# Value sums of the last four chunks moved behind all their scores, values landing in pieces, and wider rows of wo

## Chip, cores, metric

The kernel runs on one core of one Trainium2 chip. The metric is device microseconds, median of several runs. Runs of one kernel agree to about 1 to 3 us of 1955, so a difference of one microsecond needs the trace beside the time, and the profile's span is about 2 us shorter than the time that is quoted.

In the lines of a profile, PE is TensorE's matmuls, PEld the weight loads for them, DVE is VectorE, ACT ScalarE. The chain is the work that ended last, followed back to what released each step. The granted clock is the share of its full clock that PE gets: 1.00 is full, 0.50 half.

## The reference

One token attends with 32 heads of width 192 over a cache of 32,768 keys and values per head, then comes a small dense layer. What matters:

```
q      = layernorm(x) @ wq                      # 32 heads x 192
scores = q . k_cache * 192**-0.5                # k_cache: 32 x 32768 x 192, bf16, 403 MB
p      = softmax(scores)
o      = p . v_cache                            # v_cache: another 403 MB
h      = x + concat(o) @ wo                     # wo: 6144 x 640
out    = h + relu(layernorm(h) @ w1) @ w2
```

Nearly all of the work is to read 825 MB once.

## The kernel before

Keys and values come in loads of 64 rows per partition, each worked off in two chunks of 32. Of each chunk, 20 (or fewer) rows are scored on PE, for which they are transposed and copied out of PSUM by ScalarE; VectorE scores the others. The last head ends with smaller loads of 40, 16 and 8 rows, that is chunks of 20, 20, 16 and 8, called **a, b, c, d** below. The code is shortened: `...` marks what is left out between functions, and lines inside them are left out too.

```python
full = [(JL, [(J, 20), (J, 20)])] * (Sk // (P * JL))
ends = full[:-1] + [(40, [(20, 12), (20, 12)]), (16, [(16, 10)]), (8, [(8, 4)])]
NEND = 3
...
wo_view = A_wo.rearrange("(b p) n -> p b n", p=P)          # rows of 640 bf16 = 1280 B
...
def transposes(g):                                          # PE, then ScalarE
    for b0 in range(0, NB, 8):
        for b in range(nb): nc.tensor.transpose(out=tp[:, b, :], in_=kt[...], identity=ident_b[:])
        nc.scalar.copy(out=kT[:, b0:b0 + nb, :], in_=tp[:, 0:nb, :])
def scores_pe(g):                                           # PE (sp), then exp on ScalarE -> pB
def scores_dve(g):                                          # VectorE; exp_dve(g) makes pA on ScalarE
def pv(g):                                                  # value sums: matmuls with two rows each
    for i, j in enumerate(order):
        nc.tensor.matmul(o[:], lhsT=p, rhs=vt[:, (c0 + j) * Dh:(c0 + j + 2) * Dh], ...)
...
def o_scale(h):    # even heads fill columns 0..191 of o_pair, odd heads 192..383
    nc.vector.tensor_scalar_mul(out=dst[:, 0, n0:n0 + Dh], in0=o[:, 0:Dh], scalar1=s[0:2, 1:2])
    nc.scalar.activation(out=dst[:, 1, n0:n0 + Dh], in_=o[:, Dh:2 * Dh], func=F.Copy, scale=s[0:2, 1:2])
def o_turn(h):     # row -> column, once for two heads
    for b in range(3):
        for i in range(2):
            nc.tensor.matmul(ps[:, b:b + 1], lhsT=src[:, i, b * P:(b + 1) * P], rhs=ident_f[0:2, i:i + 1], ...)
...
for g in range(G):
    ...
    transposes(g)
    if g > 0:
        pv(g - 1)
    scores_pe(g)
    sc = scores_dve(g)
    ...
    exp_dve(g, sc)
den_mm(H - 1); den_rec(H - 1)
pv(G - 1)
o_scale(H - 1); o_turn(H - 1); project(H // 2 - 1)
# layernorm, w1, relu, w2, store
```

So a chunk's value sum stands on PE between the next chunk's transposes and that chunk's scores.

The softmax here doesn't subtract the row's maximum and nothing guards it: scores larger than these inputs give would overflow.

## Time and profile before

| | before |
|---|---|
| time, median of 3 runs | 1954.45 us |
| span of the profiled run | 1952.3 us |
| PE starts on the last full key load (it waits for its landing) | 1912.12 |
| PE starts on a | 1925.38 |
| den product starts (all probabilities are there) | 1939.51 |
| last value sum ends | 1940.65 |
| wo projection starts | 1942.67 |

The rows below the second are read on the timeline of PE, in us. The den product is the matmul that adds up the probabilities of a head, by which the value sums are then divided; the turn (`o_turn`, tile oT_ps) brings two heads' results from rows into columns for wo. The lines that carry the reading are in the prediction: the page shows that the transfers are the bound up to the end, and the chain shows what follows the last of them. The table cuts that end into stages.

### The profile page before, as it was taken

Reading aid. Unit: us, or ns where it says so; the run is one execution under the profiler, and the core shown is the slowest. Engines: PE = TensorE matmul, PEld = TensorE weight load, DVE = VectorE, ACT = ScalarE, POOL = GpSimd, SP = SyncE. Lnnn points to the kernel's source line nnn. Section 1 sums busy time; section 2 is a strip of 40 time slices with the busy share of each in tenths; the row PEclk is TensorE's granted clock in tenths of the full one; section 3 lists DMA queues with packets and bytes.
Section 4 is the critical chain, followed back from the end, with each engine's and each line's share of the span. In section 5 each row is a group of like instructions: output and inputs, shape, how many; then the busy total and the mean of one; then the engine's idle time right before and its main releaser. Section 6 shows DMA issues by size and latency. Waiting matters only on the chain.

```text
span 1952.3 us, 44906 instructions
## 1 busy us (share of the span) xinstructions
PE 1594.4 (82%) x20392; PEld 1122.4 (57%) x20392; DVE 1338.0 (69%) x654; ACT 1067.5 (55%) x2223; POOL 0.7 (0%) x6
## 2 busy tenths in 40 slices
PE   6887887878788788787888877888788887887887
PEld 4655565555556556555555655655555565565655
DVE  5766777667666676676767666777666766676675
ACT  4555555555555555555655555555555555555554
POOL 0000000000000000000000000000000000000000
PEclk9989889989998889998988989899899989898998
DMA  9999999999999999999999999999999999999996
GB/s 405 431 429 429 430 431 430 429 429 431 431 430 428 430 431 430 431 429 431 430 429 430 429 431 430 430 431 424 431 431 428 425 421 431 427 430 426 430 421 253
DMA packets 51522, 827.85 MB, mean 424 GB/s; under 512 B 4612, under 2 KB 17412, under 8 KB 18564
## 3 DMA queue, kind: packets, MB, share of 16 engines
q1 hardware_dynamic: 51332, 824.99, 99.0%
q8 instruction: 159, 2.61, 0.5%
q14 instruction: 31, 0.25, 0.0%
HBM read 824.97 MB, written 0.00 MB: 423 GB/s over the span
## 4 chain that ended last, share of the span: by engine, by line
DMA 77%; PE 17%; ACT 4%; DVE 1%; issue 1%; SPq 0%; ACTq 0%
DMA kt<-in_A_k_cache_dram 75%; PE o_ps L293 8%; PE tp L239 6%; ACT kT L240 3%; DMA vt<-in_A_v_cache_dram 1%; DVE pr L266 1%; PE sp L249 1%; PE sp L253 1%; PE sp L251 1%; PE qps L205 0%; ACT pA L276 0%; ACT pB L256 0%; DVE o_pair L314 0%; PE oT_ps L327 0%; ACT row_e L208 0%
## 5 line engine op out<-in xcount | busy, mean ns | idle before, releaser
L240 ACT COPY kT<-tp 128x1024 bf16<-128x1024 bf16 (+1 forms) x1025 | 905.2, 966 | 343.1 <-PE tp L239 340.2
L266 DVE TENSOR_TENSOR pr<-kt,qb 128x2304 f32<-128x2304 bf16 (+1 forms) x258 | 655.0, 2539 | 483.3 <-DMA kt<-in_A_k_cache_dram 479.9
L239 PE MATMUL tp<-ident_b,kt 128*128 128x128 bf16 x7677 | 599.3, 242 | 342.8 <-DMA kt<-in_A_k_cache_dram 269.7
L239 PEld LDWEIGHTS <-kt 128*128 128x128 bf16 x7677 | 531.1, 110 | 381.2 <-DMA kt<-in_A_k_cache_dram 280.2
L269 DVE TENSOR_REDUCE sc<-pr 128x12 f32<-128x2304 f32 (+1 forms) x258 | 654.3, 2536 | 27.6 <-ACT kT L240 1.4
L293 PE MATMUL o_ps<-vt,pB 128*2 128x384 bf16 x2559 | 498.8, 346 | 2.6 <-DMA vt<-in_A_v_cache_dram 2.6
L293 PEld LDWEIGHTS <-pB 128*2 128x2 bf16 x2559 | 203.8, 87 | 226.9 <-issue 65.9
L256 ACT ACTIVATE pB<-sp 128x20 bf16<-128x20 f32 (+1 forms) x258 | 48.4, 188 | 492.4 <-PE sp L253 492.4
L293 PE MATMUL o_ps<-vt,pA 128*2 128x384 bf16 x1537 | 291.9, 326 | 0.0
L249 PEld LDWEIGHTS <-kT 128*128 128x128 bf16 x2559 | 196.1, 96 | 85.7 <-issue 84.7
L249 PE MATMUL sp<-qm,kT 128*128 128x2 bf16 x2559 | 218.6, 164 | 0.5 <-ACT kT L240 0.5
L251 PE MATMUL sp<-qm,kT 128*128 128x1 bf16 x2559 | 215.0, 163 | 0.0
L253 PE MATMUL sp<-qm,kT 128*128 128x1 bf16 x2559 | 215.0, 163 | 0.0
L251 PEld LDWEIGHTS <-kT 128*128 128x128 bf16 x2559 | 198.7, 96 | 0.0
L293 PEld LDWEIGHTS <-pA 128*2 128x2 bf16 x1537 | 129.1, 84 | 120.8
L253 PEld LDWEIGHTS <-kT 128*128 128x128 bf16 x2559 | 197.4, 96 | 0.0
L276 ACT ACTIVATE pA<-sc 128x12 bf16<-128x12 f32 (+1 forms) x258 | 52.8, 205 | 0.0
L256 ACT ACTIVATION_READ_ACCUMULATOR pB<-sp 128x1 f32 x258 | 50.1, 194 | 0.0
L276 ACT ACTIVATION_READ_ACCUMULATOR pA<-sc 128x1 f32 x258 | 49.3, 191 | 0.0
L305 DVE TENSOR_REDUCE rec<-den 128x1 f32<-128x20 f32 x32 | 5.7, 179 | 60.2 <-PE den L299 60.2
L315 ACT ACTIVATE o_pair<-o_ps,rec 2x192 f32<-2x192 f32 x32 | 13.2, 412 | 26.9 <-DVE o_pair L314 26.9
L327 PE MATMUL oT_ps<-ident_f,o_pair 2*128 2x1 f32 x192 | 24.2, 247 | 0.1
(60 smaller groups left out, 191.4 us busy)
## 6 DMA issues: line engine op xcount, KB each, us to landing
kt<-in_A_k_cache_dram SPq DMA_DIRECT2D x127, 3072.0 KB, 35.7
vt<-in_A_v_cache_dram SPq DMA_DIRECT2D x127, 3072.0 KB, 31.4
wq<-in_A_wq_dram SPq DMA_DIRECT2D x8, 960.0 KB, 34.7
wo<-in_A_wo_dram SPq DMA_DIRECT2D x16, 480.0 KB, 31.2
kt<-in_A_k_cache_dram SPq DMA_DIRECT2D x1, 1920.0 KB, 30.7
vt<-in_A_v_cache_dram SPq DMA_DIRECT2D x1, 1920.0 KB, 25.4
kt<-in_B_w_dram SPq DMA_DIRECT2D x1, 1920.0 KB, 17.1
vt<-in_B_w_dram SPq DMA_DIRECT2D x2, 960.0 KB, 13.3
```

Of the source, the lines that this page charges most:

```text
L239: nc.tensor.transpose(out=tp[:, b, :], in_=kt[:, off:off + P], identity=ident_b[:])
L240: nc.scalar.copy(out=kT[:, b0:b0 + nb, :], in_=tp[:, 0:nb, :])
L249: nc.tensor.matmul(sp[:, 2 * i:2 * i + 2], lhsT=kT[:, 3 * i + 1, :], rhs=qm[:, 1:3], start=True, stop=False, skip_group_check=True)
L251: nc.tensor.matmul(sp[:, 2 * i:2 * i + 1], lhsT=kT[:, 3 * i, :], rhs=qm[:, 0:1], start=False, stop=False, skip_group_check=True)
L253: nc.tensor.matmul(sp[:, 2 * i + 1:2 * i + 2], lhsT=kT[:, 3 * i + 2, :], rhs=qm[:, 3:4], start=False, stop=True, skip_group_check=True)
L256: nc.scalar.activation(out=pB[:, 0:JP], in_=sp[:, 0:JP], func=F.Exp, scale=SCALE, accum_out=dsums[:, h, 2 * c + 1:2 * c + 2])
L266: nc.vector.tensor_tensor(out=pr[:, 0:JD, :], in0=kt[:, c0 * Dh:(c0 + JD) * Dh].rearrange("p (j d) -> p j d", d=Dh), in1=qb[:].unsqueeze(1 ...
L269: nc.vector.reduce_sum(out=sc[:, 0:JD], in_=pr[:, 0:JD, :], axis=mybir.AxisListType.X)
L276: nc.scalar.activation(out=pA[:, 0:JD], in_=sc[:, 0:JD], func=F.Exp, scale=SCALE, accum_out=dsums[:, h, 2 * c:2 * c + 1])
L293: nc.tensor.matmul(o[:], lhsT=p, rhs=vt[:, (c0 + j) * Dh:(c0 + j + 2) * Dh], start=first, stop=last)
L315: nc.scalar.activation(out=dst[:, 1, n0:n0 + Dh], in_=o[:, Dh:2 * Dh], func=F.Copy, scale=s[0:2, 1:2])
L327: nc.tensor.matmul(ps[:, b:b + 1], lhsT=src[:, i, b * P:(b + 1) * P], rhs=ident_f[0:2, i:i + 1], start=(i == 0), stop=(i == 1))
```

## The change

Its intent: no value sum shall make the scores of the last chunks wait, because ScalarE's copies and exponentials need those scores; values come early enough by halves; and wider rows of wo make fewer, cheaper packets. The core of the diff:

```diff
+    ENDS = [g for g in range(G) if chunks[g][2] >= len(loads) - NEND]
-    pcp = ctx.enter_context(tc.tile_pool(name="pcp", bufs=3))
+    pcp = ctx.enter_context(tc.tile_pool(name="pcp", bufs=6))
-    wo_view = A_wo.rearrange("(b p) n -> p b n", p=P)
+    wo_view = A_wo.rearrange("(g p b) n -> g p b n", p=P, b=3)
-        nc.sync.dma_start(out=t[:], in_=wo_view[:, 3 * pr:3 * pr + 3, :])
+        nc.sync.dma_start(out=t[:], in_=wo_view[pr])
 ...                                        (load_part: the load of a and b becomes one DMA for each)
+        for j0, j1 in parts or [(0, jl)]:
+            nc.sync.dma_start(out=t[:, j0 * Dh:j1 * Dh], in_=rows[:, j0 * Dh:j1 * Dh])
 ...                                        (o_turn)
-    nc.tensor.matmul(ps[:, b:b + 1], lhsT=src[:, i, b * P:(b + 1) * P], ...
+    nc.tensor.matmul(ps[:, b:b + 1], lhsT=src[:, i, b:3 * P:3], ...
 ...
-            if g > 0:
+            if g > 0 and g - 1 not in ENDS:
                 pv(g - 1)
 ...
-        pv(G - 1)
+        for g in ENDS:
+            pv(g)
```

A partition now holds three neighbouring rows of wo, so the turn must pick every third column.

More of the change, by code (lines that the diff above doesn't have):

```diff
@@ L112, in load_wo, with load_part @@
         t = wop.tile([P, 3, D], bf16, name="wo")
-        nc.sync.dma_start(out=t[:], in_=wo_view[:, 3 * pr:3 * pr + 3, :])
+        nc.sync.dma_start(out=t[:], in_=wo_view[pr])
         wo_t[pr] = t
-    def load_part(ld, src, pool, tag, name):
+    def load_part(ld, src, pool, tag, name, parts=None):
         h, k0, jl = loads[ld]
@@ L122, in load_part @@
         t = pool.tile([P, size], bf16, tag=tag, name=name)
-        nc.sync.dma_start(out=t[:, 0:jl * Dh], in_=src[h, k0:k0 + P * jl, :].rearrange("(p j) d -> p (j d)", p=P))
+        rows = src[h, k0:k0 + P * jl, :].rearrange("(p j) d -> p (j d)", p=P)
+        for j0, j1 in parts or [(0, jl)]:
+            nc.sync.dma_start(out=t[:, j0 * Dh:j1 * Dh], in_=rows[:, j0 * Dh:j1 * Dh])
         return t
@@ L129, in load_v @@
     def load_v(ld):
-        vt_t[ld] = load_part(ld, v_hd, vpool, "vt", "vt")
+        parts = [(q[3], q[3] + q[4]) for q in chunks if q[2] == ld] if ld >= len(loads) - NEND else None
+        vt_t[ld] = load_part(ld, v_hd, vpool, "vt", "vt", parts)
     w_t = {}
@@ L326, in o_turn @@
                 for i in range(2):
-                    nc.tensor.matmul(ps[:, b:b + 1], lhsT=src[:, i, b * P:(b + 1) * P], rhs=ident_f[0:2, i:i + 1],
+                    nc.tensor.matmul(ps[:, b:b + 1], lhsT=src[:, i, b:3 * P:3], rhs=ident_f[0:2, i:i + 1],
                                      start=(i == 0), stop=(i == 1))
```

## The prediction

> **What bounds the kernel now.** I read the profile page first, for the whole span, and then only the last 60 us, because all but one part of the change touches only those.
>
> ```profile
> DMA  9999999999999999999999999999999999999996
> ...
> q1 hardware_dynamic: 51332, 824.99, 99.0%
> ...
> DMA kt<-in_A_k_cache_dram 75%; PE o_ps L293 8%; PE tp L239 6%; ACT kT L240 3%; DMA vt<-in_A_v_cache_dram 1%; DVE pr L266 1%; PE sp L249 1%; PE sp L253 1%; PE sp L251 1%; PE qps L205 0%; ACT pA L276 0%; ACT pB L256 0%; DVE o_pair L314 0%; PE oT_ps L327 0%; ACT row_e L208 0%
> ```
>
> The reader is to see that the 16 DMA engines are 90% busy or more in every slice but the last, that one queue takes 99% of their time, and that loads of keys make 75% of the chain that ended last. 825 MB must come in, and the engines only have to keep up. So outside the end, only what makes the transfers cheaper can shorten the run. The end is different. I call the last four chunks, of 20, 20, 16 and 8 rows per partition, a, b, c and d. From the chain of work that ended last, in order of time (start, us, what):
>
> ```profile
> 1906.10 25.42 DMA vt<-in_A_v_cache_dram
> 1931.52 0.04 issue
> 1931.56 1.78 PE o_ps L293 x10
> ...
> 1933.88 0.86 PE tp L239 x15
> 1934.74 1.72 PE o_ps L293 x10
> ...
> 1936.91 0.36 PE tp L239 x6
> 1937.27 0.00 issue
> 1937.27 1.46 PE o_ps L293 x8
> ...
> 1939.51 0.40 PE den L299 x2
> 1939.91 0.75 PE o_ps L293 x4
> ```
>
> Their value sums (o_ps) have 10, 10, 8 and 4 matmuls, and all four are in the fence. The first waits until the values of a and b, one transfer, land at 1931.52, but PE had been idle for it only 0.76 us, says the timeline of PE. After it, sums, transposes and scores take turns on PE. The last sum ends at 1940.65 (its last group starts at 1940.16 and takes 0.49), and a chain of small steps from there ends the kernel.
>
> What ScalarE does between is as important (timeline of ScalarE, start, us):
>
> ```profile
> 1930.34 2.21 ACT L240 COPY kT<-tp 128x1024 bf16<-128x1024 bf16 x3
> 1933.92 0.18 ACT L256 ACTIVATE pB<-sp 128x12 bf16<-128x12 f32 x1 [1.38 <-PE sp L253]
> ...
> 1934.44 1.82 ACT L240 COPY kT<-tp 128x1024 bf16<-128x1024 bf16 x2
> 1936.95 0.18 ACT L256 ACTIVATE pB<-sp 128x10 bf16<-128x10 f32 x1 [0.69 <-PE sp L253]
> ...
> 1937.36 0.80 ACT L240 COPY kT<-tp 128x768 bf16<-128x768 bf16 x1
> 1939.01 0.17 ACT L256 ACTIVATE pB<-sp 128x4 bf16<-128x4 f32 x1 [0.84 <-PE sp L253]
> ```
>
> The copies of b, c and d (2.21, 1.82, 0.80 us) must run one after another, each followed by scores on PE and two exponentials, before the next. ScalarE idles only 1.38, 0.69 and 0.84 us before the three exponentials. So the old order already puts the sums of a, b and c largely under the copies of b, c and d.
>
> **What the Trainium skill says.** "TensorE: Matmul & The Clock Gate", section "Part 2: What happens when you issue a matmul": matmuls stay in program order, only weight loads are pulled ahead. So a sum placed after d's scores can't fill a gap before them. The trace agrees: PE sat 0.76 us on the late values with transposes of a later chunk to do. The same page, "Part 1: The HAM clock gate", says that the clock halves after an idle window of about 3.4 us and comes back after a busy one. The trace agrees, with partly idle windows enough (stretch, us; PE busy; later columns include the granted clock):
>
> ```profile
> 1907.00:1910.40 3.40, 1.74 (x36) 1.08 (x34) 0.81 (x1) 0.67 (x5) 0.00 (x0) 0.99 1.00 408
> 1910.40:1917.20 6.80, 5.08 (x36) 3.83 (x37) 4.92 (x2) 3.55 (x4) 0.00 (x0) 0.50 0.78 334
> 1930.80:1934.20 3.40, 2.64 (x38) 1.68 (x38) 3.26 (x3) 2.02 (x7) 0.00 (x0) 1.00 0.91 337
> 1934.20:1937.60 3.40, 3.40 (x44) 2.00 (x42) 2.04 (x3) 2.64 (x9) 0.00 (x0) 1.00 0.95 323
> ```
>
> A stretch with PE busy 1.74 of 3.40 us is followed by half clock (0.50); one with 2.64 of 3.40 is not. "DMA: Bandwidth & Descriptors", section "Why small descriptors are slow (HBM only)", says that each packet has a fixed overhead of about 3 cycles, so small rows lose a little. In the trace's single packets, 1280 B take a median of 55 ns and 3072 B take 121: per byte, the small ones cost 9% more.
>
> **The change part by part.**
>
> 1. Rows of wo. Each of 16 loads goes from 384 packets of 1280 B to 128 of 3840 B; an engine has 24, then 8. By the median packet times, 24 x 55 = 1.32 us, and 8 x 149 = 1.19 us (149 interpolated between 121 for 3072 B and 234 for 6144 B): 0.13 us a load, 2 us in all. But the stream waits for its slowest engine, and in the landing records of the trace a wo load adds 1.17 us to the last engine's landing, against 7.26 us for a load of 3072 KB, so 1.13 us for wo's share of bytes. That leaves 0.04 us a load, 0.6 us in all. Between 0.6 and 2, I choose **-1.0 us**; it is in the stream, so it moves everything after it.
>
> 2. Values in four pieces. The two sizes that were one transfer (a, b) are split, so one more transfer, same bytes. It would bring a's values forward by half of 4.5 us, but in the new order no sum is asked for until d's exponentials. All values have landed by 1934.4 in the old trace (landing records), before that. **0 us.** More buffers for the probabilities hold the four waiting chunks and cost nothing. The strided weights of the turn (6 tiny matmuls at the end) I take as free.
>
> 3. Scores first. On PE the sums leave the gaps, and all of a to d's 32 matmuls come after the den product. In the old trace's times: copies of b end at 1930.34 + 2.21 = 1932.55. The scores follow each copy at once, so the last are out by 1932.8, b's exponentials start at about 1932.85 (old: 1933.92), and copies of c 0.53 us after them (the old distance, 1933.92 to 1934.44), at 1933.38. They end at 1935.20; scores, 0.4; exponentials at 1935.63; copy of d 1936.16 to 1936.96; exponentials 1937.33 to 1937.78; den at 1937.83 (old 1939.51). VectorE does not hold this up: its scores of d end at 1936.37 in the old trace. So the chain of scores gains **1.7 us**. Then the sums start at 1938.16 and take 32 x 0.161 us (six matmuls took 1931.56 to 1932.53) plus 0.17 for the last one's drain: 5.33 us, end 1943.49, against 1940.65. Net **+2.8 us** at full clock: 28 matmuls, 4.5 us, came out from under the copies, and 1.7 us of score time was gained.
>
> 4. The clock. From 1930.8 to 1938.2 PE now has only b's scores, c's transposes and scores, d's, and den: about 0.6 + 1.0 + 0.55 + 0.5 + 0.3 + 0.3 = 3.2 of 7.4 us, or 44%. In the windows above, 1.74 of 3.40 (51%) led to half clock. So I expect the burst of sums to begin at half clock, 0.32 us a matmul, until one busy window is over: 2.2 to 5.6 us at half speed, by where the window falls, costing half of that, 1.1 to 2.8, in the mean 1.9; and 0.4 in slower transposes and scores. With a chance of 4 in 5, (1.9 + 0.4) x 0.8 = **+1.8 us**.
>
> Sum: 1954.45 - 1.0 + 2.8 + 1.8 = 1958.05. Because a shift of the stream can also free the last full load's first chunk from the half clock of 1910.4 to 1917.2, which would bring the end forward by up to 1.2 us (PE began a's transposes at 1925.38, 1.2 after its keys landed), I take off a little: **1957.8 us**.
>
> **Rivals.**
> - The end gains. If the old order were held up mostly by late values, scores first would take that wait away, some 2 us. For it: the chain does name the value load, at 1931.52. Against: PE's wait there is 0.76 us, and ScalarE was copying until 1932.55 anyway. It would make 1952 to 1953.
> - The stream gains more: if small rows cost what the single packets say, or more, -2 to -2.5 us, and with no cold clock the end costs 2.8: about 1955. Speaking for it is the packet time, against it the landings.
> - A new end by the last weights: w2's second half lands at 1944.1 in the old trace, needed at 1947.5. The end grows, so it has more slack, not less. Hidden anyway: 0.
> - The clock stays full through the gap: 1956.2.
>
> **Range and chances.** All of it is a few us of 1954, and 2% is 39 us, so same is near certain: faster 0.01, same 0.98, slower 0.01. Low, 1954.8: full clock and the stream's best; high, 1960.2: the longest cold burst and no gain from wo. In the range 8 in 10.
>
> **What would show it.** (a) wo: the first stretch of the tail (the landing of the last full key load, 1912.1) earlier by about 1 us. (b) Sums: 32 matmuls of o_ps in a row on PE with nothing between, starting 1.7 us or so earlier than the last sum did, and ending near 3 us later at full clock. (c) ScalarE's wait before b's exponentials gone from 1.38 to about 0.3. (d) A granted clock of 0.5 at the start of the burst, or 0.32 us a matmul. The prediction is wrong if PE's gap before den is filled, if the clock stays up, or if the landing moves by more than 2.5 us; it would be wrong in sign if the value wait had held the end.

## The result, and the profile after

The changed kernel took 1958.96 us (median of 4 runs, 1958.19 to 1959.44), the kernel before 1954.24 us beside it (4 runs, 1953.99 to 1954.61). The ratio is 1.0024, with a 95% interval of 1.0006 to 1.0041. The loss is a quarter of a per cent: "same" at 2%, and 1.2 us over the predicted 1957.8, within its range.

The chain of the changed kernel, from the den product on (start, us, what):

```profile
1937.22 0.62 PE den L303 x2
1937.84 6.54 PE o_ps L297 x32
1944.38 0.03 issue
1944.41 0.42 DVE o_pair L318
1944.83 0.04 issue
1944.87 2.36 PE oT_ps L331 x12
```

All 32 matmuls of the value sums now stand in one piece at the end, after the den product, and last 6.54 us; before, only the last 4 stood there. The den product itself came earlier. And the turn (oT_ps), 0.84 us for 6 passes in the chain before, is 2.36 us for 12. The kernel before, same stage, from the end of its last sum:

```profile
1940.68 0.42 DVE o_pair L314
1941.10 0.02 issue
1941.12 0.42 ACT o_pair L315
1941.55 0.04 issue
1941.59 0.84 PE oT_ps L327 x6
```

The timeline of ScalarE in the changed kernel shows that the intent was reached: it waited 0.32 us for b's scores, not 1.38, and 0.44 and 0.41 for those of c and d.

```profile
1932.01 0.18 ACT L260 ACTIVATE pB<-sp 128x12 bf16<-128x12 f32 x1 [0.32 <-PE sp L257]
1934.79 0.18 ACT L260 ACTIVATE pB<-sp 128x10 bf16<-128x10 f32 x1 [0.44 <-PE sp L257]
1936.72 0.17 ACT L260 ACTIVATE pB<-sp 128x4 bf16<-128x4 f32 x1 [0.41 <-PE sp L257]
```

Stages in the two profiled runs, from the same starts as in the table above:

| stage | before, us | after, us | difference |
|---|---|---|---|
| up to PE's start on the last full key load | 1912.12 | 1911.19 | -0.93 |
| from there to PE's start on a | 13.26 | 13.35 | +0.09 |
| a to den product | 14.13 | 12.68 | -1.45 |
| den product to the end of the last sum | 1.14 | 7.15 | +6.01 |
| end of the last sum to wo projection | 2.02 | 3.10 | +1.08 |
| wo projection to the end | 9.63 | 9.93 | +0.30 |
| span | 1952.3 | 1957.4 | +5.1 |

The scores gained 1.45 us, and the sums that stood under them came out at 6.01. How much of that is the order and how much a slower clock, and why the turn got longer, the experiments tell apart.

### The profile page after: what moved, and what is told of

It is laid out like the page before. It is cut to its first block, busy times and chain, and to the rows that moved or that the text cites. A ratio compares the mean times of both kernels' runs of the same rounds, so it can differ in the third digit from the quotient of the medians.

```text
span 1957.4 us, 44907 instructions
## 1 busy us (share of the span) xinstructions
PE 1609.1 (82%) x20392; PEld 1136.1 (58%) x20392; DVE 1336.8 (68%) x654; ACT 1067.3 (55%) x2223; POOL 0.7 (0%) x6
## 4 chain that ended last, share of the span: by engine, by line
DMA 73%; PE 20%; ACT 4%; DVE 2%; issue 1%; SPq 0%; ACTq 0%
DMA kt<-in_A_k_cache_dram 73%; PE o_ps L297 9%; PE tp L243 7%; ACT kT L244 3%; DVE pr L270 1%; PE sp L253 1%; PE sp L257 1%; PE sp L255 1%; PE oT_ps L331 1%; ACT pA L280 0%; ACT pB L260 0%; DVE o_pair L318 0%; PE qps L209 0%; PE den L303 0%; PE attT L341 0%
## 5 line engine op out<-in xcount | busy, mean ns | idle before, releaser
L331 PE MATMUL oT_ps<-ident_f,o_pair 2*128 2x1 f32 x192 | 36.3, 311 | 0.5 <-DVE o_pair L318 0.5
L331 PEld LDWEIGHTS oT_ps<-ident_f,o_pair 2*128 2x128 f32 x192 | 34.9, 257 | 1.2 <-DVE o_pair L318 0.9
```

The costliest lines, as they stand in the source:

```text
L331: nc.tensor.matmul(ps[:, b:b + 1], lhsT=src[:, i, b:3 * P:3], rhs=ident_f[0:2, i:i + 1], start=(i == 0), stop=(i == 1))
```

## Experiments

**Theory.** The change is a sum of four parts: the stream gains about 1 us from wo; the order costs about 2.8 us, because the sums leave gaps that ScalarE's copies made; PE, with those gaps empty, falls to half clock, and the burst of sums begins slow; and the turn is 1 us longer. **Rivals.** The order is harmless, and the other parts make the loss; or the burst is slow because it waits for values; or the turn is only slow because of the clock; or the stream's gain never reaches the end.

Each kernel ran five times, unless said otherwise (before 3 times in its own row, after 4), beside the kernel before on the same chip. The "from a" column is what the profiled run took from PE's start on a to the end of the span; it leaves out how the last full load met the clock (below).

| run | what it is | median us | before beside it | ratio (95%) | from a, us |
|---|---|---|---|---|---|
| before | | 1954.45 | | | 26.9 |
| after | the change | 1958.96 | 1954.24 | 1.0024 (1.0006 to 1.0041) | 32.9 |
| e1_order | new order alone | 1958.63 | 1954.62 | 1.0022 (1.001 to 1.0035) | 32.0 |
| e2_wo | wo rows alone | 1954.86 | 1954.62 | 1.0002 (0.999 to 1.0015) | 28.9 |
| e3_pieces | value pieces alone | 1953.43 | 1954.62 | 0.9994 (0.9981 to 1.0006) | 26.6 |
| e4_fill | the change, gaps filled | 1957.13 | 1954.62 | 1.0014 (1.0 to 1.0027) | 30.9 |
| e5_last_old | the change, old last turn | 1958.24 | 1954.49 | 1.0018 (1.0004 to 1.0032) | 33.2 |
| e6_best | old order, both other parts, old last turn | 1951.34 | 1954.49 | 0.9985 (0.9972 to 0.9999) | 26.2 |
| e7_fill_last_old | the change, gaps filled, old last turn | 1955.33 (4 runs) | 1954.49 | 1.0004 (0.999 to 1.0018) | 29.9 |
| e8_wo_last_old | wo rows alone, old last turn | 1953.17 | 1954.49 | 0.9996 (0.9984 to 1.0009) | 28.0 |

### One part at a time

**e1_order** keeps only the parts of the diff around ENDS and the six buffers.

> The new order of the last four chunks alone; wo rows of 1280 B, values of a and b in one transfer. Theory (the order alone costs more than the whole change does, because the cheaper wo rows give some back): the end of the last value sum 4.65 us later after the landing of the last full key load than before, small steps at half clock another 0.3, no gain in the stream: about 1959.2 us, that is +5.0. The turn of the heads takes about 0.9 us after ScalarE's scaling, as before. Rival (the strided turn or the split values make the loss, not the order): at most +3, 1957.

It took 1958.63 us, 4.0 above the kernel before in its rounds; expected was 5.0, and the rival had said 3 at most. Its trace has the burst of 32 sums at 6.73 us after the den product and the turn at 0.84 us, as before the change. So the order alone, with the slow clock that it brings, makes 4.0 us where the whole change lost 4.7.

**e2_wo** keeps only `wo_view`, `load_wo` and the turn's `b:3 * P:3`.

> Rows of wo of 3840 B alone, with the strided turn that they need. Theory: the stream ends 0.9 us earlier (landing of the last full key load, as in the changed kernel) and the last turn takes 1.0 us longer (all 12 passes now need both heads' halves and ScalarE's; before, 4 of them ran ahead), so nothing is left: 1954.3 us, within 0.4 of before. Rival (the turn is free, as predicted): 1953.3. Rival (no gain in the stream): 1955.3.

It took 1954.86 us, 0.24 above the kernel before: gain and loss cancel, though the time is 0.6 above what the theory named. The trace shows both. PE started on the last full load at 1911.23, 0.9 earlier, and the turn stands in its chain with 2.36 us for 12 passes:

```profile
1940.08 2.36 PE oT_ps L327 x12
```

Here the granted clock is 1.00 during the turn, so its length is not the clock's. Two more stages differ in this profile and nearly cancel: from the last full load to a it took 12.49 us in place of 13.26, and PE then waited 1.35 us for a's values in place of 0.76.

**e3_pieces** keeps only the `parts` of load_part and load_v.

> Values in four pieces alone, old order. Theory: chunk a's values land 2.3 us earlier (about 1929.2 in the old trace's time), PE's wait of 0.76 us before a's sum goes, and the rest moves up by as much: 1953.4 us, -0.8. Rival (ScalarE's copies bound the end, values are hidden): 1954.2, no change.

It took 1953.43 us, 1.2 below. The interval includes no change, but the trace shows the step: from the start on a to the den product it took 13.30 us in place of 14.13, because a's sum no longer waits for values. This part of the change helps in the old order. In the new one nobody asks for values that early: from a to the den product e1, without pieces, took 12.69 us and the changed kernel, with them, 12.68.

### The clock

**e4_fill** is the changed kernel with dummy matmuls in PE's gaps, whose result nobody reads; the outputs stay right.

```diff
+        def fill(n):
+            d = mm_bank([P, 384], f32, "fill")
+            for _ in range(n):
+                nc.tensor.matmul(d[:], lhsT=ident_b[:], rhs=wo_t[H // 2 - 1][:, 0, 0:384], start=True, stop=True)
             transposes(g)
+            if g in ENDS[1:]:
+                fill({1: 5, 2: 5, 3: 3}[ENDS.index(g)])
             scores_pe(g)
...
+        fill(3)
         den_mm(H - 1)
```

> The changed kernel with 16 dummy matmuls of 128x384 (5, 5, 3 and 3; result unused) in PE's gaps among the last four chunks. Theory (the gaps let the clock fall to half, and the burst of 32 sums starts cold): clock stays at 1.0, the 32 sums take 5.3 us in place of 6.5, scores come 0.2 us sooner: 1957.5 us, 1.4 below the changed kernel although PE does 2.6 us more work. Rival (the burst is slow for another reason, such as values or probabilities being waited for): 6.5 us again and 1959 or more.

It took 1957.13 us: with more work on PE, 1.8 us below the changed kernel's median. The profiled runs differ by 3.0 us (1957.4 to 1954.4): 1.49 between the start of the den product and the end of the sums, 0.21 in the scores before, 0.21 in the end steps, 0.24 up to the last full load, and 0.84 from there to a (12.51 in place of 13.35 us), which the dummies do not touch (see e6_best). These are stretches of the changed kernel (columns: stretch, its us, then busy us of PE, PEld, VectorE, ScalarE and GpSimd, each with its count; the granted clock; DMA share; GB/s), first from b's transposes to the den product, then the beginning and the rest of the burst:

```profile
1929.90:1937.20 7.30, 3.47 (x61) 2.70 (x60) 5.29 (x5) 5.77 (x18) 0.00 (x0) 0.75 0.95 337
1937.80:1940.70 2.90, 2.90 (x12) 1.19 (x12) 0.34 (x2) 0.00 (x0) 0.00 (x0) 0.56 0.52 189
1940.70:1944.40 3.70, 3.67 (x23) 1.70 (x21) 0.00 (x0) 0.00 (x0) 0.00 (x0) 1.00 0.22 82
```

and the same for e4_fill, gaps and burst:

```profile
1928.90:1935.90 7.00, 5.44 (x76) 3.49 (x75) 6.06 (x5) 5.66 (x18) 0.00 (x0) 1.00 0.89 317
1936.20:1941.60 5.40, 5.39 (x33) 2.60 (x32) 0.34 (x2) 0.00 (x0) 0.00 (x0) 1.00 0.59 220
```

With PE busy for 3.47 of 7.30 us the clock fell to half (it was 0.50 from 1933.5 to 1940.3) and the burst began so, with 12 matmuls in 2.90 us; with 5.44 of 7.00 it stayed full and all 32 sums took 5.30 us in the chain, against 6.54. The rival, that the burst waits for values or probabilities, falls: nothing about either was changed.

### The turn

**e5_last_old** is the changed kernel, but the last pair of heads keeps the old rows of wo and the old turn.

```diff
-        nc.sync.dma_start(out=t[:], in_=wo_view[pr])
+        nc.sync.dma_start(out=t[:], in_=wo_view[pr] if pr < H // 2 - 1 else wo_old[:, 3 * pr:3 * pr + 3, :])
-                    nc.tensor.matmul(..., lhsT=src[:, i, b:3 * P:3], ...)
+                    nc.tensor.matmul(..., lhsT=src[:, i, b:3 * P:3] if pr < H // 2 - 1 else src[:, i, b * P:(b + 1) * P], ...)
```

> The changed kernel, but the last pair of heads loads its wo rows in the old layout and so has the old, unstrided turn. Theory (the last turn cost 1.07 us because all its passes wait for both heads and each is slower): the turn ends about 0.9 us after ScalarE's scaling in place of 2.4 us after VectorE's; 1957.9 us, 1.0 below the changed kernel (1959.0). Rival (the turn's time is hidden, or is the half clock's): 1959.

The median of 1958.24 us is 0.7 below the changed kernel, with single runs from 1957.38 to 1958.91, so the times alone do not settle it. The trace does: the turn is 0.84 us again, and the stage from the last sum to the projection is 2.02 in place of 3.10 us. But in the profiled run, the slowest of the five, the burst stayed at half clock for longer and gave it back:

```profile
1936.90:1943.00 6.10, 6.10 (x20) 2.41 (x21) 0.34 (x2) 0.00 (x0) 0.00 (x0) 0.50 0.40 146
1943.10:1945.30 2.20, 2.20 (x15) 1.02 (x12) 0.00 (x0) 0.00 (x0) 0.00 (x0) 1.00 0.00 0
```

Twenty records fall in 6.1 us at half clock; in the changed kernel's profiled run the first 2.5 us of the burst were at half clock. How long the burst stays slow thus differs from run to run, by 1.7 us here (8.22 us of sums in its chain, against 6.54). What sets it is not shown: e5's clock stayed at half after a stretch of 3.40 us with PE busy for 3.14 (from 1936.2), the changed kernel's rose after one with 3.08 (from 1936.9).

Why the turn is longer, two views tell. In the groups by line, one load of its weights takes longer when every third column is picked (before, then after; mean ns is the second number after the bar):

```profile
L327 PEld LDWEIGHTS oT_ps<-ident_f,o_pair 2*128 2x128 f32 x192 | 22.7, 186 | 0.8 <-DVE rec L306 0.3 <-ACT o_pair L315 0.2
```

```profile
L331 PEld LDWEIGHTS oT_ps<-ident_f,o_pair 2*128 2x128 f32 x192 | 34.9, 257 | 1.2 <-DVE o_pair L318 0.9
```

The layout does this and not the order: the median of these loads is 187 ns in e1_order, with old rows, and 256 in e2_wo, with new ones.

And by the code, the old turn's first column (b = 0) holds only columns 0 to 127, all from the even head, scaled long before; its 4 passes (an fp32 matmul is two in these records) run while the odd head is being scaled. The changed turn mixes both heads in every column, so nothing runs ahead; most of its 12 passes stand behind ScalarE, not 6. The timeline of PE agrees: the old turn's first matmul is at 1940.58, before the last scaling began; the new one's at 1944.87, after VectorE's. The two effects together are 1.08 us. What each is worth alone was not tried; an estimate from the timelines of the weight loads (the old turn's last 6 in 0.74 us, the new turn's 12 in 2.26) gives about 0.5 us for the four more passes behind ScalarE and 0.6 for the slower loads of ten.

### What is left, and the best of the parts

**e7_fill_last_old** is e4_fill with e5's change: the order, without the cold clock and without the longer turn.

> The changed kernel with both costs taken away that are not the order itself: dummy matmuls in the gaps (clock stays full) and the old turn for the last pair. Theory: what is left is the order's own 2.8 us less 0.9 of the stream, so 1956.1 us, about +1.7 to +2 over before. Rival (the order itself is free once the clock is full): 1953.5.

It took 1955.33 us, 0.8 above the kernel before although the stream gains about 1. From the start on a to the end of the last sum it took 18.12 us (1923.41 to 1941.53), against 15.27 before (1925.38 to 1940.65). So at full clock the changed end costs 2.85 us more than the kernel before, about 0.1 of it because the den product stands behind the last dummies (it starts 0.17 us after the last exponential, in the kernel before 0.06). Scores and sums follow each other in its chain like this:

```profile
1935.87 0.37 PE den L309 x2
1936.24 5.30 PE o_ps L303 x32
```

The rival, that the order is free once the clock is full, falls. The 2.85 us are measured against an end that still waited 0.76 us for values. Against the old order with pieces (e3 and e6, both 14.44 us over the same stretch) the order costs 3.68: the sums in the gaps had made the scores 0.84 us longer (13.30 against 12.46), and stand behind them now with 4.5.

**e8_wo_last_old** is e2_wo with e5's change.

> Only the 3840 B rows of wo, for all pairs but the last, old order. Theory: the stream's gain is kept and the last turn is the old one: 1953.6 us, -0.9. Rival (what the rows gain in the stream does not reach the end): 1954.5.

It took 1953.17 us, 1.3 below; expected was 0.9 below, and the interval includes no change. Start on the last full load at 1910.78 and a turn of the old length agree with the theory; its stage from the last full load to a is one of the short ones (12.49 us, see e6_best).

**e6_best** is e8_wo_last_old with e3's pieces: everything of the change but the order, and the old last turn.

> Old order; values in four pieces; 3840 B rows of wo for all pairs but the last. Theory: the gains of the parts add up, -0.9 from the stream and -1.0 from the pieces: 1952.7 us, faster than both kernels, clock full to the last sum. Rival (the parts share one wait, so only the larger counts): 1953.5.

It took 1951.34 us (1950.86 to 1952.91), 3.2 below the kernel before and 7.6 below the changed one: it beats both, by little (0.15% against the kernel before; the interval just leaves out no change). Its chain has the sums back between transposes and scores, with full clock to the last of them:

```profile
1930.89 0.86 PE tp L243 x15
1931.75 1.72 PE o_ps L297 x10
...
1936.52 0.40 PE den L303 x2
1936.92 0.75 PE o_ps L297 x4
```

The gain is larger than the 1.8 expected. 0.85 us of it is a stage that nobody had changed: from the last full load to a, its profiled run took 12.41 us, the kernel before 13.26. In all ten profiles the clock falls to half near the start of that stage, around the end of PE's wait for the load. In before, after, e1, e3 and e5 it fell 0.9 to 1.7 us before PE's start, stayed at half for 6.8 us, and the stage took 13.3 to 13.7 us. In e2, e4, e6, e7 and e8 it fell between 0.1 us before PE's start and 1.4 us after it, stayed for 3.4 us, and the stage took 12.4 to 12.7. All five short ones have the new rows of wo, but so have after and e5, and each kernel was profiled once: whether this is chance, or the earlier load helps, stays open. Without pieces it gains little, because PE then only waits longer for a's values (1.64 us in e8, whose stage from a to den took 15.01). The rest of e6's gain in the profile is 1.31 us in the stream and 0.83 by the pieces.

## Why the prediction was right, and where it was off

The prediction summed to +3.35 us, the profiled runs show +5.10. Term by term:

| term | predicted | shown |
|---|---|---|
| stream, by wo rows | -1.0 | -0.93 |
| last full load to a | -0.25 | +0.09 |
| order at full clock | +2.8 | +2.85 (e7) |
| half clock in scores and burst | +1.8 | +1.71 (1.90 in e1, 3.39 in e5) |
| values in pieces, within the new order | 0 | -0.01 (a to den, after against e1) |
| turn with strided weights | 0 | +1.08 |
| end steps after the turn | 0 | +0.30 |

- **The stream** was right in size, though the prediction had chosen it between two readings, 0.6 and 2. Single runs scatter: with 3840 B rows PE started on the last full load between 1910.44 and 1911.23 (seven profiled runs, mean 1910.9), with 1280 B rows between 1911.87 and 1912.12 (three, mean 1912.0).
- **The last full load to a**: the 0.25 us that the prediction took off for a shorter half clock were not there (13.35 us after, 13.26 before). Five other runs with the new rows do show a shorter one.
- **The order** was right in mechanism and size: a shorter chain of scores, and 28 matmuls that came out from under ScalarE's copies. That a later sum cannot fill an earlier gap on PE shows best in the changed kernel: PE stood idle for 0.77 us before 1933.60, though a's values had landed at 1928.46 and its probabilities were done at 1929.42; its sum still came after the den product. The 1.71 us in the row on half clock is the difference of the changed kernel's 19.83 us (1924.54 to 1944.37, from the start on a to the end of the sums) to e7's 18.12.
- **The clock**: the prediction gave a cold burst a chance of 4 in 5, and it was cold in the three traces that have the new order and unfilled gaps (after, e1, e5), and in neither with filled ones: at half clock for the first 2.5, 2.8 and 5.9 us, where the prediction had 2.2 to 5.6.
- **The turn** is the step that failed, in the prediction's words "The strided weights of the turn (6 tiny matmuls at the end) I take as free." They were not: 2.36 us for 0.84 in the chain. It looked at the count of matmuls, not at what each waits for, nor at how the weights are read. The profiled runs came out 1.75 us above the prediction's sum: 1.08 by this term, 0.34 by the gain before a that did not come, 0.30 by the end steps; the rest evens out. Of the 0.30 us in the end steps, 0.2 is the layernorm's matmul (0.57 in place of 0.37 us); e3, in the old order and with the old turn, has 0.57 as well, so it does not take the change to bring this.
- **The rivals**: "the end gains" falls by e1. It was true only of the pieces: the value wait of 0.76 us was real, and e3 collected it without the new order. The last weights of the dense layer stayed hidden, as predicted: no wait for them is in the chain of any run.

## What to carry to other kernels

When PE and ScalarE take turns on a chain, work put on PE while ScalarE copies is mostly hidden (here 4.5 us of sums cost 0.84), and the same work collected behind the chain is paid in full and, after gaps like these, begins at half clock; first look whose wait the reordering ends. If an early wait is for data, split the transfer before moving the work. And a new layout of a weight is paid where its partner is read: check what its strided operand waits for, and whether an early part can still run ahead.

## What the Trainium skill lacked or had wrong

- "TensorE: Matmul & The Clock Gate", "Part 1": the clock is told to halve after an idle window of about 3.4 us and to return after a busy one; the page also tells of a kernel whose short pauses made it swing, but gives no share of busy time at which it turns. Here it halved after a stretch with PE busy for 1.72 of 3.40 us (after, from 1930.1) and stayed full at 5.44 of 7.00 (e4). It rose after 3.08 of 3.40 in the changed kernel, and not after 3.14 of 3.40 in e5.
- "SBUF — State Buffer", the note on 16-byte lines under "Door 1: The DMA port swizzle (why `[64,N]` ≈ `[32,N]`)": it gives 4 fp32 values as how far one can stride for free, which can be read as free for a step of 3. It also asks for two hits on a line, which a step of 12 B does not always give, so it does not contradict the trace; but it names no cost. Weight loads of 2 x 128 fp32 values with a step of 3 took 257 ns, without a step 186.
- "DMA: Bandwidth & Descriptors", "Why small descriptors are slow (HBM only)": its one example is a descriptor of 256 B. An estimate from its fixed cost of about 3 cycles per packet, with 32 B a cycle, makes three packets of 1280 B 5% dearer than one of 3840 B. In the traces they are 11% dearer (medians of 55 and 149 ns), and widening the rows brought 0.93 us over 16 loads of 480 KB.
